# Backward of a transformer block on one Trainium2 core: joined loads, re-timed transposes, another order of the tail

## The chip, the core and the metric

The kernel runs on one core of one Trainium2 chip. The metric is the device time of one execution in microseconds (us). The core has a matrix engine (PE), a vector engine (DVE), an activation engine (ACT), a general engine (POOL) and SP, whose queue issues most of the DMAs here. All five run beside each other and wait for one another by semaphores. Matrix products land in PSUM, which DVE and ACT empty.

## What is computed

The reference is a block y = x + attention(norm(x)) + ffn(norm(x)) and the gradients of all its inputs for a given grad_out. There are 2048 rows of 448 columns, 16 heads of 28 columns, and an FFN of 1792 columns; all is bf16.

```
xn = layernorm(x)
q, k, v = split(xn @ wqkv)
p = softmax(q k^T / sqrt(28));  o = p v
y = x + o @ wo + (silu(xn @ w_gate) * (xn @ w_up)) @ w_down
outputs: y, d/dx, d/dwqkv, d/dwo, d/dw_gate, d/dw_up, d/dw_down
```

Output 1 is the input gradient d/dx, output 2 the gradient of w_qkv.

## The kernel before

A head's 28 columns are padded to 32 (HP), so four heads fill the 128 partitions; such a four is a *group* (G = 4 groups), and half of it, two heads on 64 partitions, is a *pair* (8 pairs). The rows come in 16 tiles of 128 (NT).

**Forward stage** (L255 to L624). Layer norm, then for each group and each block of 512 queries the exponentials of the scores and their product with v; the FFN, its gradients and the next group's projections are queued as filler for PE between the steps, each with a cost, and worked off at an even pace (`fill`, L308). `proj_done` (L198) writes a group's transposed q, k and v to DRAM with three POOL DMAs of 128 partitions. `do` (L496), the tail of a group's block, makes the gradient of the head outputs, divided by the softmax sum, transposes it with a DMA and writes it to DRAM (L524). At the end of the stage `load_pair(0, 1)` and `load_group(0, 1, ...)` bring in what the next stage needs first.

**Backward attention** (L641 to L917) is one loop over 512 *units* and 16 steps more. A unit is one pair, one block of 512 keys (kc) and one tile of 128 queries; eight units are a *window* (UW = 8, window number W, place in it pos). Step k of the loop does, in the order of the code:

- PE: scores of unit k (L851, q's first 64 partitions with k's) and dP of unit k-1 (L862, the last 64 partitions: dO with v). Both go to `sd` tiles, 3 buffers of two PSUM banks.
- ACT: E = exp(scores) (L869). DVE: ds = dP * E (L880), in one of 8 `ds` buffers.
- ds must also be had transposed, as `dsT` of the window. For six of eight units SP issues a DMA transpose (L882). The two units named in TQ (1 and 4) are transposed by PE into the PSUM tile `aux` (`pe_transpose`, L770) and copied out (`tr_out`, L778): unit 1 at pos 6 of its window, with the copy on DVE at once; unit 4 at pos 0 of the next window, with the copy on ACT behind that step's E.
- PE: `acc_mm(k-3)` (L738) adds unit k-3 to the gradients of v and k of the key block; after the last one ACT empties it (L754), SP transposes it (L761), POOL writes it to `dqkv_d` (L763).
- At pos 5, `dq_mm(W-2)` (L784) multiplies the dsT of two windows before with k, into `aux`; at pos 6 DVE adds the result up (`dq_out`, L799). After the fourth key block it is transposed (L817) and written (L820).
- Each window has a *job* for PE, spread over pos 1 to 4 into the single `aux` bank: an output tile of y, a tile of one of the two FFN parts of d/dx (written to pA_d and pB_d), or a part of the w_qkv gradient of a finished group (`dwq_mms`, L669: xn tiles as the stationary operand, the gradients of q, k, v as the moving one, four chunks of 128 columns of d). `job_out` empties it at pos 4. The chunk that a job reads is loaded by SP two windows before, at pos 0 (L660, L666).

Other loads are issued by SP at pos 4 (L840 to L846): from three lists, `pload` (the next pair, eight loads: q, k, dO and v, 64 partitions each, in two halves), `gload` (the next group, six loads) and `wload` (weights), it takes up to 2, 1 and 2 in each window. `load_pair` (L545) fills two tiles of 128 partitions for a pair: q above dO, and k above v.

**Tail** (L898 to L981). The last group's w_qkv gradient is begun at step N + UW + 5 with the key and value products of 12 tiles for four chunks; the rest follows behind the loop, then its q part, each chunk copied out by ACT, packed by POOL and written (L688). Then for each of 16 tiles of d/dx: PE sums pA, pB (L956) and 12 products of the q, k, v gradients with w_qkv (L958); ACT copies it with a row sum (L962), DVE makes the second sum and two scalars bb and cc (L965 to L971), ACT scales it into t1 (L974), DVE adds cc * xn to get t2 (L976), POOL adds grad_out (L979), SP stores it (L980). `load_c` (L929) brings in pA, pB, grad_out and `dqkv_d` by chunks of two or four tiles, first by SP, later by ACT.

Of the kernel before, what the change touches and what calls it, by code (L numbers as in the profile page):

```python
# [17 lines left out]
S = 2048  # L18
# [19 lines left out]
def kernel(  # L38
# [27 lines left out]
    qT_d = dram.tile([G, P, S], BF16, name="qT_d")  # L66
    kT_d = dram.tile([G, P, S], BF16, name="kT_d")
    vT_d = dram.tile([G, P, S], BF16, name="vT_d")
    dOT_d = dram.tile([G, P, S], BF16, name="dOT_d")
# [396 lines left out]
    def o_items(g, qc, o_ps):  # L466
# [29 lines left out]
        def do(i):  # L496
# [27 lines left out]
            pool.dma_start(out=dOT_d[g, :, qc * 512:(qc + 1) * 512], in_=dT[:])  # L524
# [20 lines left out]
    def load_pair(pr, parts):  # L545

        g, r = pr // 2, 64 * (pr % 2)
# [4 lines left out]
        return [lambda i=i, dst=dst, r0=r0, src=src: sp.dma_start(  # L552
                    out=dst[r0:r0 + 64, i:i + n], in_=src[g, r:r + 64, i:i + n])
                for r0, srcs in ((0, (qT_d, kT_d)), (64, (dOT_d, vT_d)))
                for dst, src in zip((q, k), srcs) for i in range(0, S, n)]
# [73 lines left out]
    outp = cst.enter_context(tc.tile_pool(name="outp", bufs=2))  # L629
    ps_sd = cst.enter_context(tc.tile_pool(name="ps_sd", bufs=3, space=PSUM))  # L630
# [137 lines left out]
    TQ = (1, 4)  # L768
# [9 lines left out]
    def tr_out(eng):  # L778

        ps, dst = st["tr"]  # L780
        out, in_ = dst.rearrange("p j c q -> p (j c) q"), ps[:]
        act.copy(out=out, in_=in_) if eng is act else dve.tensor_copy(out=out, in_=in_)  # L782
# [45 lines left out]
    dps = {}  # L828
    fillers, last_dwq = [], []
    for k in range(N + 2 * UW):  # L830
        W, pos = k // UW, k % UW
        if k < N:
            pr, kc, w, qi = units[k]
            if k % 64 == 3 and pr + 1 < NPR:
                pload.extend(load_pair(pr + 1, 2))
            if k % 128 == 3 and pr + 2 < NPR:
                gload.extend(load_group(pr // 2 + 1, 2, vp if pr // 2 % 2 else ksp))
            if pos == 0:
                job_load(W + 2)
            if pos == 4:  # L840
                if W == len(jobs) - 1:
                    wload.extend(load_w("wq", 2))
                for lst, n in ((pload, 2), (gload, 1), (wload, 2)):
                    for f in lst[:n]:
                        f()
                    del lst[:n]  # L846
            q, kv = qd[pr]
            qt = 8 * w + qi
            s_ps = ps_sd.tile([P, 2, 512], FP32, name="sd")
            for j in range(2):  # L850
                pe.matmul(s_ps[:, j, :], lhsT=q[HP * j:HP * j + HP, qt * P:(qt + 1) * P],  # L851
                          rhs=kv[HP * j:HP * j + HP, kc * 512:(kc + 1) * 512],
                          start=True, stop=True, tile_position=(HP * j, 0))
        late_tr = pos == 0 and 1 <= W <= NW
# [15 lines left out]
        if late_tr:  # L870
            tr_out(act)
# [15 lines left out]
        if pos == 1:  # L887
            if 3 <= k < N + 3:
                acc_mm(k - 3)
            if job:  # L890
                st["aux"] = ps_x.tile([P, 512], FP32, name="aux")
                fillers = job_mms(W, st["aux"])
        if 1 <= pos < 5 and job:
            n = -(-len(fillers) // (5 - pos))
            for f in fillers[:n]:
                f()
            fillers = fillers[n:]
        if k == N + UW + 5:  # L898
            for c in range(4):
                if c % 2 == 0:  # L900
                    g_t = ps_sd.tile([P, 2, 512], FP32, name="sd")
                last_dwq.append((g_t[:, c % 2, :], dwq_mms(3, c, g_t[:, c % 2, :])))
            for _, m in last_dwq:
                for f in m[0][:12]:
                    f()
# [3 lines left out]
        if pos != 1 and 3 <= k < N + 3:  # L909
            acc_mm(k - 3)  # L910
        if pos == 4 and job:
            job_out(W, st["aux"])
        if pos == 6 and W < NW:
            pe_transpose(W, TQ[0])
            tr_out(dve)
    while sp_later:
        sp_later.pop(0)()  # L917
    ast.close()


    with ExitStack() as fin:
        ckf = fin.enter_context(tc.tile_pool(name="ckf", bufs=5))
        wk = fin.enter_context(tc.tile_pool(name="wk", bufs=3))
        one = fin.enter_context(tc.tile_pool(name="one", bufs=1))
        dy_t = one.tile([P, NT, D], BF16, name="dy_t")
        pab = [one.tile([P, NT, D], BF16, name=f"pab{i}") for i in range(2)]
        dq_c = {}

        def load_c(ck, q):  # L929

            if ck >= NT // 2:
                return
            if ck % 2 == 0:
                ts = slice(2 * ck, 2 * ck + 4)
                for i, src in enumerate((pA_d, pB_d)):
                    q.dma_start(out=pab[i][:, ts, :], in_=src[:, ts, :])
                act.dma_start(out=dy_t[:, ts, :], in_=dy_d[:, ts, :])
            dq_c[ck] = ckf.tile([P, 3 * G, 2 * P], BF16, name="dq_c")
            q.dma_start(out=dq_c[ck][:], in_=dqkv_d[ck])
        for ck in range(3):  # L940
            load_c(ck, sp)
        for part in range(2):
            for c, (ps, m) in enumerate(last_dwq):
                for f in m[part][12 * (1 - part):]:
                    f()
                if part == 1:
                    dwq_out(3, c, ps)
        wq = wtile["wq"]
        for t in range(NT):
            if t % 2 == 0:  # L950
                load_c(t // 2 + 3, act)
            cks = dq_c[t // 2]
            g_t = ps_sd.tile([P, 2, 512], FP32, name="sd")
            g_ps = g_t[:, 0, :D]
            for i in range(2):
                pe.matmul(g_ps, lhsT=ident_bf[:], rhs=pab[i][:, t, :], start=(i == 0), stop=False)  # L956
            for n in range(3 * G):
                pe.matmul(g_ps, lhsT=cks[:, n, (t % 2) * P:(t % 2 + 1) * P], rhs=wq[:, n, :],  # L958
                          start=False, stop=(n == 3 * G - 1))
# [15 lines left out]
            t2 = wk.tile([P, D], FP32, name="t2")  # L975
            dve.scalar_tensor_tensor(out=t2[:], in0=xn_sp[:, t, :D], scalar=cc[:, 0:1], in1=t1[:],  # L976
                                     op0=ALU.mult, op1=ALU.add)
            dx = wk.tile([P, D], BF16, name="dx")
            pool.tensor_tensor(out=dx[:], in0=t2[:], in1=dy_t[:, t, :], op=ALU.add)  # L979
            sp.dma_start(out=out1_d[:, t, :], in_=dx[:])  # L980
# [31 lines left out]
```

## Time and profile before

| | us |
|---|---|
| three runs | 1529.53, 1534.82, 1534.94; median 1534.82 |
| the profiled execution, its own time | 1534.68 |
| its span (first to last instruction) | 1532.9 |
| forward stage, to about | 645 |
| backward attention, from there to about | 1457 |
| tail, from there to the end | 1532.9 |

| engine | busy us | share of the span |
|---|---|---|
| PE (matrix products) | 1414.2 | 92% |
| ACT | 1187.9 | 77% |
| DVE | 1100.7 | 72% |
| POOL | 395.0 | 26% |

The views read are: sums of busy time over stretches; waits (who waited for whom, in total, number of times, longest); the timeline (start, duration, engine, line, what is written and read, and in brackets the idle time before it and what ended it); and the chain of work that ended last, followed back in time. PE's matmuls are pipelined and their ends modelled, so a PE that is busy 97% may still have waits on the chain. Rows of SP are those of its queue: the time that it takes to issue a DMA, not that of the transfer; how long a transfer took to land is told apart. L numbers are lines of the kernel.

### The profile page before, as it was taken

Reading aid. Unit: us, or ns where it says so; the run is one execution under the profiler, and the core shown is the slowest. Engines: PE = TensorE matmul, PEld = TensorE weight load, DVE = VectorE, ACT = ScalarE, POOL = GpSimd, SP = SyncE. Lnnn points to the kernel's source line nnn. Section 1 sums busy time; section 2 is a strip of 40 time slices with the busy share of each in tenths; the row PEclk is TensorE's granted clock in tenths of the full one; section 3 lists DMA queues with packets and bytes.
Section 4 is the critical chain, followed back from the end, with each engine's and each line's share of the span. In section 5 each row is a group of like instructions: output and inputs, shape, how many; then the busy total and the mean of one; then the engine's idle time right before and its main releaser. Section 6 shows DMA issues by size and latency. Waiting matters only on the chain.

```text
span 1532.9 us, 32019 instructions
## 1 busy us (share of the span) xinstructions
PE 1414.2 (92%) x12176; PEld 600.1 (39%) x12176; DVE 1100.7 (72%) x1421; ACT 1187.9 (77%) x1333; POOL 395.0 (26%) x664
## 2 busy tenths in 40 slices
PE   6899999999999999798989988989899899999987
PEld 3233333333333333333334344334345343544353
DVE  7664555656666667377878878888788788888925
ACT  6898998889888888576767777778778778788823
POOL 4332443344435444400111121101112101111033
PEclk9999999999999999889999999999999999999999
DMA  9976767878877799799999999999999999999984
GB/s 216 190 157 144 156 122 157 171 136 169 173 166 144 159 190 214 178 197 208 218 206 207 185 194 209 197 204 206 208 195 197 198 205 183 180 190 211 186 272 140
DMA packets 682106, 285.12 MB, mean 186 GB/s; under 512 B 637136, under 2 KB 650464, under 8 KB 681952
## 3 DMA queue, kind: packets, MB, share of 16 engines
q1 hardware_dynamic: 652016, 210.03, 75.5%
q0 software_dynamic: 25968, 64.53, 17.2%
q10 hardware_dynamic: 3968, 8.52, 1.7%
q8 instruction: 95, 1.56, 0.4%
q14 instruction: 59, 0.48, 0.1%
HBM read 67.34 MB, written 63.44 MB: 85 GB/s over the span
## 4 chain that ended last, share of the span: by engine, by line
PE 59%; ACT 13%; DMA 12%; DVE 8%; issue 6%; POOL 1%; SPq 0%; DVEq 0%; ACTq 0%; POOLq 0%
DMA dsT<-ds 9%; PE f_ps L356 8%; PE s_ps L599 7%; PE f_ps L382 7%; PE sd L851 6%; ACT E L869 5%; PE aux L718 5%; PE acc L748 4%; PE o_ps L581 4%; ACT eT L604 4%; PE aux L775 4%; DVE ds L880 4%; PE aux L795 3%; ACT dsT L782 3%; PE f_ps L180 3%
## 5 line engine op out<-in xcount | busy, mean ns | idle before, releaser
L880 DVE TENSOR_TENSOR ds<-sd,E 128x1024 bf16<-128x1024 f32 x512 | 611.5, 1219 | 134.0 <-PE sd L862 49.8
L869 ACT ACTIVATE E<-sd 128x1024 bf16<-128x1024 f32 x512 | 516.7, 1023 | 175.6 <-PE sd L862 136.5
L604 ACT ACTIVATE eT<-s_ps 128x1024 bf16<-128x1024 f32 x512 | 497.2, 1025 | 79.5 <-PE s_ps L599 76.1
L862 PE MATMUL sd<-kT,qT 32*128 32x512 bf16 x1024 | 203.4, 390 | 22.2 <-ACT E L869 21.3
L851 PE MATMUL sd<-kT,qT 32*128 32x512 bf16 x1024 | 202.7, 392 | 20.6 <-DVE ds L880 18.0
L748 PE MATMUL acc<-ds,v_sp 128*32 128x512 bf16 x1024 | 205.3, 396 | 0.7 <-DVE ds L880 0.7
L748 PE MATMUL acc<-E,O_sp 128*32 128x512 bf16 x1024 | 205.1, 396 | 0.2 <-ACT dkv_o L754 0.2
L599 PE MATMUL s_ps<-qT,kT 32*128 32x512 bf16 x1024 | 152.8, 383 | 10.1 <-ACT eT L604 7.9
L421 POOL DMA_DIRECT2D hd_d<-fT x168 | 126.9, 773 | 18.5 <-DVE fT L416 5.3
L382 PE MATMUL f_ps<-xnT,wgu 128*128 128x512 bf16 x448 | 117.6, 381 | 1.7 <-DVE w_sb L408 1.5
L763 POOL DMA_DIRECT2D dqkv_d<-dkv_o x64 | 39.2, 616 | 293.3 <-ACT dkv_o L754 291.4
L718 PE MATMUL aux<-W,ck 128*128 128x448 bf16 x448 | 107.5, 357 | 3.3
L851 PEld LDWEIGHTS <-qT 32*128 32x128 bf16 x1024 | 51.2, 91 | 150.0 <-issue 141.2
L581 PE MATMUL o_ps<-eT,v_sp 128*32 128x512 bf16 x1024 | 102.8, 391 | 0.0
L356 PE MATMUL f_ps<-xn_sp,f_sp 128*128 128x448 bf16 x448 | 99.7, 356 | 0.0
L599 PEld LDWEIGHTS <-kT 32*128 32x128 bf16 x1024 | 42.4, 90 | 143.5 <-issue 136.8
L748 PEld LDWEIGHTS <-O_sp 128*32 128x32 bf16 x1024 | 50.3, 93 | 113.5 <-issue 104.0
L775 PE MATMUL aux<-ident_bf,ds 128*128 128x128 bf16 x1024 | 81.3, 224 | 13.5 <-DVE dq_acc L807 6.5
L356 PEld LDWEIGHTS <-f_sp 128*128 128x128 bf16 x672 | 58.3, 98 | 78.6 <-issue 23.5
L862 PEld LDWEIGHTS <-qT 32*128 32x128 bf16 x1024 | 65.2, 91 | 60.5 <-issue 56.5
L775 PEld LDWEIGHTS <-ds 128*128 128x128 bf16 x1024 | 63.5, 99 | 42.4 <-issue 41.7
L394 DVE SCALAR_TENSOR_TENSOR g<-t_sb,f_ps 128x512 f32<-128x512 f32 x56 | 38.4, 686 | 54.0 <-ACT t_sb L392 53.9
(133 smaller groups left out, 1763.1 us busy)
## 6 DMA issues: line engine op xcount, KB each, us to landing
hd_d<-fT POOLq DMA_DIRECT2D x168, 128.0 KB, 4.6
ck<-hd_d SPq DMA_DIRECT2D x32, 448.0 KB, 4.3
ck<-hd_d SPq DMA_DIRECT2D x16, 576.0 KB, 4.9
dsT<-ds SPq DMA_TRANSPOSE x384, 4.2
dqkv_d<-dkv_o POOLq DMA_DIRECT2D x64, 64.0 KB, 3.8
dq_c<-dqkv_d ACTq DMA_DIRECT2D x5, 768.0 KB, 6.1
W<-wT_d SPq DMA_DIRECT2D x14, 224.0 KB, 3.6
out_dram<-dw_o POOLq DMA_DIRECT2D x28, 96.0 KB, 3.7
```

Source lines behind the costliest of these rows:

```text
L356: pe.matmul(acc[:, :D], lhsT=src[:, 12 * (t // 4) + 4 * wi + t % 4, :], rhs=rhs[:, t, :D], start=(t == 0), stop=(t == NT - 1))
L382: pe.matmul(st[name][:], lhsT=w(c), rhs=src[:, tsl, c, :], start=(c == 0), stop=(c == 3))
L581: pe.matmul(o_ps[HP * hh:HP * (hh + 1), :], lhsT=v[:, kt, HP * hh:HP * (hh + 1)], rhs=e[hh // 2][:, hh % 2, :], start=(kt == 0), stop=(kt ...
L599: pe.matmul(s_ps[:, j, :], lhsT=kT[r:r + HP, kt * P:(kt + 1) * P], rhs=qT[r:r + HP, qc * 512:(qc + 1) * 512], start=True, stop=True, tile_ ...
L604: act.activation(out=e[:], in_=s_ps[:], func=ACT.Exp, scale=SCALE)
L718: return [lambda n=n: pe.matmul(ps[:, :D], lhsT=t[:, n, :], rhs=w[:, n, :], start=(n == 0), stop=(n == NFC - 1)) for n in range(NFC)]
L748: pe.matmul(acc[r:r + HP, :], lhsT=src[:, qt, 64 * hp + HP * j:64 * hp + HP * j + HP], rhs=m[:, j, :], start=(qt == 0), stop=(qt == NT - 1 ...
L775: pe.transpose(ps[:, i, :], ds[:, i // 4, (i % 4) * P:(i % 4 + 1) * P], ident_bf[:])
L851: pe.matmul(s_ps[:, j, :], lhsT=q[HP * j:HP * j + HP, qt * P:(qt + 1) * P], rhs=kv[HP * j:HP * j + HP, kc * 512:(kc + 1) * 512], start=Tru ...
L862: pe.matmul(d_ps[:, j, :], lhsT=q[r:r + HP, qt * P:(qt + 1) * P], rhs=kv[r:r + HP, kc * 512:(kc + 1) * 512], start=True, stop=True, tile_p ...
L869: act.activation(out=E[k][:], in_=s_ps[:], func=ACT.Exp, scale=SCALE)
L880: dve.tensor_tensor(out=DS[k - 1][:], in0=d_ps[:], in1=E[k - 1][:], op=ALU.mult)
```

## The change

Four places, beside each other in one diff:

1. **Copies and loads of pairs.** The DRAM tensors qT_d, dOT_d, kT_d and vT_d become two, laid out by pair as the loads want them: qdo_d (q above dO) and kv_d (k above v). `proj_done` writes them with six DMAs of 64 partitions for three of 128, `do` with two for one. `load_pair` takes four loads of 128 partitions instead of eight of 64. At pos 4 the loop takes one pair load in even windows and one group load in odd ones.
2. **Transposes by PE.** TQ becomes (2, 6). Unit 2 is still transposed at pos 6, its copy comes a step later, at pos 7 behind ds; unit 6 is transposed at pos 1 of the next window, and DVE copies it ahead of ds. ACT copies no dsT any more.
3. **The job** begins at pos 2 and is spread over three positions instead of four.
4. **The tail.** The last w_qkv gradient is made with the operands exchanged: the gradients of q, k, v are the stationary operand, xn (448 columns) the moving one, so that three PSUM tiles hold it transposed; three DMA transposes turn it back, POOL packs it with five copies, four DMAs write it. Its Q part (64 products of 32 columns in four strips) comes behind the first two tiles of d/dx. pA and pB of the first four tiles are loaded in the last window, chunk 0 of dqkv_d right behind the loop. In the loop over tiles, t2, the addition of grad_out and the store of a tile come one tile later (`finish`), and the last three additions run on DVE.

The diff, cut to its core:

```diff
-    qT_d = dram.tile([G, P, S], BF16, name="qT_d")
...
+    qdo_d = dram.tile([2 * G, P, S], BF16, name="qdo_d")
+    kv_d = dram.tile([2 * G, P, S], BF16, name="kv_d")
...
-        pool.dma_start(out=vT_d[g], in_=vT[:])
-        pool.dma_start(out=qT_d[g], in_=qT[:])
-        pool.dma_start(out=kT_d[g], in_=kT[:])
+        for hp in range(2):
+            rows = slice(64 * hp, 64 * hp + 64)
+            for dst, src in ((kv_d[2 * g + hp, 64:], vT), (qdo_d[2 * g + hp, :64], qT), (kv_d[2 * g + hp, :64], kT)):
+                pool.dma_start(out=dst, in_=src[rows, :])
...
-        return [lambda i=i, dst=dst, r0=r0, src=src: sp.dma_start(
-                    out=dst[r0:r0 + 64, i:i + n], in_=src[g, r:r + 64, i:i + n])
-                for r0, srcs in ((0, (qT_d, kT_d)), (64, (dOT_d, vT_d)))
-                for dst, src in zip((q, k), srcs) for i in range(0, S, n)]
+        return [lambda i=i, dst=dst, src=src: sp.dma_start(out=dst[:, i:i + n], in_=src[pr, :, i:i + n])
+                for i in range(0, S, n) for dst, src in ((q, qdo_d), (k, kv_d))]
...
-    TQ = (1, 4)
+    TQ = (2, 6)
...
+                if W == NW - 1:
+                    load_sums(0, sp, prep)
...
-                for lst, n in ((pload, 2), (gload, 1), (wload, 2)):
+                for lst, n in ((pload, 1 - W % 2), (gload, W % 2), (wload, 2)):
...
-        late_tr = pos == 0 and 1 <= W <= NW
+        late_tr = pos == 1 and 1 <= W <= NW
...
-            tr_out(act)
+            tr_out()
...
+        if pos == 7 and W < NW:
+            tr_out()
+        acc = 3 <= k < N + 3
+        if pos == 2 and job:
+            st["aux"] = ps_x.tile([P, 512], FP32, name="aux")
+            fillers = job_mms(W, st["aux"])
+        lump = []
+        if 2 <= pos < 5 and job:
             n = -(-len(fillers) // (5 - pos))
+            lump, fillers = fillers[:n], fillers[n:]
...
+        def kv(t):
+            pe.matmul(ps, lhsT=dsp[2 * G - 2 + c][0][:, t, :], rhs=xn_sp[:, t, :D],
+                      start=(t == 0), stop=(t == NT - 1))
+
+        def q(t):
+            for h in range(4):
+                pe.matmul(ps[HP * h:HP * (h + 1)],
+                          lhsT=dsp[2 * G - 2 + h // 2][1][:, t // 8, t % 4, t % 8 // 4,
+                                                          HP * (h % 2):HP * (h % 2 + 1)],
+                          rhs=xn_sp[:, t, :D], start=(t == 0), stop=(t == NT - 1),
+                          tile_position=(0, HP * h), skip_group_check=True)
...
+        for t in range(2):
+            dx_mms(t, first[t])
+        q_t = ps_sd.tile([P, 2, 512], FP32, name="sd")
+        for f in last_dwq(2, q_t[:, 0, :D]):
+            f()
...
+            add = pool if t < NT - 3 else dve
+            add.tensor_tensor(out=dx[:], in0=t2[:], in1=dy_t[:, t, :], op=ALU.add)
+            sp.dma_start(out=out1_d[:, t, :], in_=dx[:])
...
+            if t > 0:
+                finish(t - 1, *held)
+            held = (t1, cc)
+        finish(NT - 1, *held)
```

More of the change, by code (lines that the diff above doesn't have):

```diff
@@ L523, in do @@
                                    in_=dOl[:].rearrange("p t c -> p (t c)"))
-            pool.dma_start(out=dOT_d[g, :, qc * 512:(qc + 1) * 512], in_=dT[:])
+            for hp in range(2):
+                pool.dma_start(out=qdo_d[2 * g + hp, 64:, qc * 512:(qc + 1) * 512],
+                               in_=dT[64 * hp:64 * hp + 64, :])
         push([[(0.2, lambda i=i: tr(i)) for i in range(4)], [(0.26, lambda i=i: do(i)) for i in range(4)]]
@@ L924 @@
         one = fin.enter_context(tc.tile_pool(name="one", bufs=1))
+        one3 = fin.enter_context(tc.tile_pool(name="one3", bufs=3))
         dy_t = one.tile([P, NT, D], BF16, name="dy_t")
[L926 to L931, printed above, removed]
-                return
[L933 to L948, printed above, removed]
-        for t in range(NT):
[L950 to L959, printed above, removed]
+        z = one.tile([P, 4, 3, 4, DH], BF16, name="dwq_z3")
@@ new lines, in dx_mms @@
+        def dx_mms(t, g_ps):
+            for i in range(2):
+                pe.matmul(g_ps, lhsT=ident_bf[:], rhs=pab[t // 4, i][:, t % 4, :], start=(i == 0), stop=False)
+            for n in range(3 * G):
+                pe.matmul(g_ps, lhsT=dq_c[t // 2][:, n, (t % 2) * P:(t % 2 + 1) * P], rhs=wq[:, n, :],
+                          start=False, stop=(n == 3 * G - 1))
+        load_dy(0)
+        for ck in range(1, 4):
+            load_dq(ck, sp, ckf)
+        load_sums(1, sp, one3)
+        for c, (ps, m) in enumerate(last):
+            for f in m[12:]:
+                f()
+            last_out(c, ps)
```

98 lines of the change are left out of this document (64 added, 34 removed).

## The prediction

> **What bounds the kernel now.** I read the stage sums first, then the waits of the backward stage, one disturbed and one quiet window in the timeline, the chain through a quiet window, and the tail. The backward stage has 64 windows of 8 units; a window's length is the distance between every eighth L880 row. It has three parts:
>
> ```profile
> 657.20:870.80 213.60, 196.25 (x1828) 82.24 (x1824) 168.83 (x160) 155.31 (x168) 22.49 (x38) 0.98 1.10 207
> 870.80:1290.30 419.50, 381.52 (x4020) 172.90 (x4016) 349.96 (x331) 320.92 (x346) 58.06 (x130) 0.98 1.08 200
> 1290.30:1445.70 155.40, 149.02 (x1620) 68.89 (x1616) 138.25 (x132) 126.14 (x137) 22.50 (x54) 0.99 1.09 190
> ```
>
> The columns are stretch, length, then busy PE, PEld, DVE, ACT and POOL. The third part (13 windows) runs at 11.95 us a window with PE busy 96%; quiet windows of the first part, whose PE job is longer, take 12.51. At those paces the first part (16 windows) would take 200.2 and the second (33) 394.4; they take 13.4 and 25.1 more. So 38.5 us are lost in windows that have something the others lack: loads of the next pair and group. The waits of that stage say who is late:
>
> ```profile
> DVE ds L880 <- DMA dsT<-ds: 46.6, 33, 3.6
> ```
>
> VectorE waits 46.6 us for transposes of old ds tiles (there are 8 buffers). One such place:
>
> ```profile
> 978.90 1.26 SPq L882 DMA_TRANSPOSE dsT<-ds  x1
> ...
> 980.25 0.53 SPq L666 DMA_DIRECT2D ck<-hd_d  x1
> ...
> 980.88 5.90 SPq L882 DMA_TRANSPOSE dsT<-ds  x3
> ...
> 986.75 1.23 DVE L880 TENSOR_TENSOR ds<-sd,E 128x1024 bf16<-128x1024 f32 x1 [1.42 <-DMA dsT<-ds]
> 986.83 1.66 SPq L552 DMA_DIRECT2D kT<-kT_d  x2
> 988.02 0.39 PE L851 MATMUL sd<-kT,qT 32*128 32x512 bf16 x2 [0.50 <-DVE ds L880]
> ```
>
> The SP queue has no gap: it is the queue that is behind. Comparing each L882 row's start with the end of the L880 row that it serves, SP lags 1 to 4 us in quiet windows, climbs to 8 in windows with pair loads, stalls VectorE there, and then works off about 1 us a window. Its work in a window at 1.36 us a transpose (start to start): 6 transposes 8.2, the transposes of dkv_o and dq_o 1.0 on average, the chunk load 0.6, held up in a row some 1 to 2: about 11.0 of 11.95. Each half-partition pair load adds 0.62, two in each of four windows; a group load adds 0.62 in six. That is more than the 0.9 left.
>
> In a quiet window the chain goes through PE and two ACT waits:
>
> ```profile
> 1373.37 1.02 ACT dsT L782
> 1374.38 0.04 issue
> 1374.43 0.92 PE aux L718 x4
> ...
> 1383.09 1.03 ACT E L869
> ...
> 1384.55 0.57 PE aux L775 x8
> 1385.12 0.02 issue
> 1385.14 1.02 ACT dsT L782
> ```
>
> The PE job of each window waits for ACT's copy of transposed ds.
>
> **The loads.** Before: 8 pair loads in the first four windows of a pair, two each, and 6 group loads, one a window. After: 4 pair loads, one in every even window, and 6 group loads in the odd ones. A load of 128 partitions by 2 KB is not in L552, but the group loads move 256 KB in one row: 0.58 us of SP, landing in 3.6. So SP's extra work falls from at most 1.9 us a window to at most 0.62, and SP gets 11.6 to do in 11.95 (12.1 with the x_c load, in 12.5). Bounds for the 38.5: all stays (if bytes, not rows, are the limit: they are the same) or all goes. I take three quarters, **-29**: the lag already falls by 1 us in a window that has 0.9 to spare. The last pair load is issued two windows before its use, with 3.6 us to land. In the forward stage POOL gets 12 + 16 more DMA rows of 0.53 to 0.62 us, 16 us in 640, where it is busy 270; PE (97%) covers it, nobody reads these tensors for 100 us. Uncovered it would cost the 16; I take 0.
>
> The Trainium skill, "DMA: Bandwidth & Descriptors", section "Rules for kernel authors", also says that two transfers to disjoint partition halves serialize and that one of 128 partitions should be used. Its section "Issuing engines are not separate DMA queues" speaks against a large gain: issue time on a sequencer is usually small relative to the DMA itself. By that the -29 would be near 0 and the time about 1522 (rival 2). The gapless SP row is against it here.
>
> **The transposes in PE.** The second one moves to position 1 of the next window, both are copied by DVE: 62 copies of 1.01 us leave ACT, 62 of 0.68 join DVE. In the row of three ds, 3.47 us, DVE takes one each 1.125 us and a copy 0.60 (1383.11 to 1383.71). DVE's own work rises from 8 x 1.125 + 0.6 + 0.6 = 10.2 to 10.8 of 11.95. PE's stays: positions without a job 0.66 (two pairs of score products 0.33, four accumulations 0.33), transposes 0.57, dQ products 1.15, the job 14 x 0.187 plus 0.12 a lump. I laid these out by hand, with PE allowed ahead until the three sd slots stop it: the order before gives 11.46, the new one 11.25 (E to product waits remain; the job waits for a copy that DVE has finished half a us before). PE's job in three lumps instead of four leaves DVE more bunched: positions 6, 7, 0, 1 hold 6.3 us of DVE work against 3.8 of PE. So a window is 6.76 (positions 2 to 5) + 6.3 - B, where B is how far DVE may lag behind PE; my layout has B near 1.8. Bounds for 62 windows: +37 (each 0.60 uncovered) to -50 (a copy wait of 0.8 gone each). By the layout -13; since SP's 11.0 to 11.6 is then close behind, I take half, **-6**. Other PE-transposed units (2, 6 for 1, 4) leave six DMA transposes in a window, as before.
>
> **The tail.** The chain before:
>
> ```profile
> 1458.92 4.89 DMA dsT<-ds
> 1463.86 1.05 PE aux L795 x14
> 1464.93 0.70 DVE dq_o L813
> 1465.65 6.62 DMA dq_sp<-dq_o
> 1472.32 0.97 PE sd L681 x15
> ```
>
> PE is idle 4.8 us for dq_sp, then works off 128 products with copies between them, and begins the input gradient at 1479.4. New: two sums (896 KB) are loaded in window 63, in front of the last transposes; at the 256 GB/s of this stretch up to 3.5 us, I take 2.5, so the last dQ products end at 1467.4 for 1464.9. Then 8 kv products (448 wide, 0.19): 1468.9. The first tile needs dq_c of chunk 0: its last write lands at 1463.6, its load takes 4.5 to 8.1 us (rows of dq_c), so 1470.5. Two tiles at 2.65: 1475.8; dq_sp has landed by then (3.5 to 6.6 us after 1468.1). The Q part, 64 products in four column strips: between 3.0 (four at once, 16 x 0.19) and 12.2 (one by one); the row L795, 16 in 1.15 us at 512 wide, gives 4.0: 1479.8. Then 14 tiles.
>
> ```profile
> 1483.46 0.15 DVE L969 SCALAR_TENSOR_TENSOR bb<-s,rstd 128x1 f32<-128x1 f32 x1
> ...
> 1518.33 1.03 POOL L979 TENSOR_TENSOR dx<-t,dy_t 128x448 bf16<-128x448 f32 x1 [1.70 <-DVE t L976]
> ...
> 1518.71 0.67 DVE L969 SCALAR_TENSOR_TENSOR bb<-s,rstd 128x1 f32<-128x1 f32 x1
> 1519.30 0.15 DVE L971 SCALAR_TENSOR_TENSOR cc<-s,rstd 128x1 f32<-128x1 f32 x1
> 1519.47 0.72 ACT L974 ACTIVATE t<-sd,bb,rstd 128x448 f32<-128x448 f32 x1 [1.48 <-DVE cc L971]
> ```
>
> While POOL adds, the tiny bb takes 0.67 instead of 0.15 and ends with it: add, bb, t1, t2, add is a ring of 2.73 us, longer than PE's 2.65, and it throttles PE by its sd slots. With t2 and the add held back a tile, POOL's add lies beside ACT's t1, the ring is about 2.4, PE sets 2.65: 14 x 2.65 = 37.1, PE ends at 1516.9 (before: 1523.05). Behind it 1.7 (g_sb, junk, bb, cc), 1.3 (t2 and add of tile 14), 1.3 (the last, add on DVE; bounds 0.6 and 1.03 by t2 and POOL's add), 2.5 for the store as now: 1523.7, against 1532.9. That is -9; POOL's new copies (between 0.18, the row of 56 elements, and 1.03 each, five of them) and four stores wait for the transposed Q part and hold tiles 1 to 3 back, I take **-7**; bounds -10 and +2 (Q part uncovered, loads late).
>
> **Sum**: profiled execution 1534.7 (span 1532.9 and 1.8 around it; the median shown is 1534.8): -29 - 6 - 7 = **1493**. Own range 1478 to 1510.
>
> **Rivals.** 1. *VectorE becomes the bound (slower).* If B is under 0.3, because every ds waits for its own product, a window is about 12.9 instead of 12.57 (788.5 us over 62 windows, less what the longer jobs add). With B = 0.1: 62 x (12.96 - 12.57) = +24, no stalls left to save, tail -7: 1552. The point is B = 0.4: below it the windows cost more than the tail gives. For it: DVE's busy share of 89%; against it: ds rows back to back with PE ahead by a unit. Chance 0.08.
> 2. *Bytes, not rows, hold SP.* The same bytes bring the same stalls: 1534.7 - 6 - 7 = 1522. For it: DMA share over 1 everywhere and an L882 row of 3.2 us with its ds ready; against it: windows with one extra load at the end of the stage run at 11.95. Chance 0.13.
> 3. *Gains and DVE cancel.* B near 0.5: windows as long as now on the mean, tail -7: 1528. Chance 0.10.
> 4. *More*: the layout's -13 and all 38.5 come through with the tail's -9: 1474 or less. Chance 0.05. That loads are not joined at all is not one: the new slice spans all partitions.
> Forecast 0.64.
>
> **Numbers.** A measurement of this kernel tells about 0.5% from no change: under 1527 is faster. Forecast, 2 and 4: 0.82. Case 3: 0.10. Case 1: 0.08. The range 1474 to 1528 leaves out rival 1 and most of rival 4.
>
> **What would show it.** Loads: the wait of ds for dsT falls from 46.6 to under 15, SP's lag stays under 6, windows of the second part near 11.9. Transposes: no dsT copy on ACT, quiet windows 11.6 to 11.9; if they are over 12.2, DVE is the bound. Tail: first dx product near 1470 in old time, bb at 0.15, tiles each 2.65. I am wrong if ds still waits for dsT, or if PE waits for ds in quiet windows.

## The result and the profile after

| | before | after |
|---|---|---|
| median of the runs | 1533.2 us | 1513.6 us (1511.0, 1511.1, 1516.2, 1516.7) |
| ratio, 95% interval | | 0.9876 [0.9844, 0.9908] |
| profiled execution, span | 1534.7, 1532.9 us | 1511.0, 1509.2 us |
| last copy of the forward stage, to the first ds | 2.2 us | 10.7 us |
| the same copy, to SP's first dsT transpose | 10.4 us | 12.0 us |
| windows 1 to 62 | 788.5 us | 760.2 us |
| tail, from the start of window 63 | 87.2 us | 84.7 us |

The change brings 19.6 us (23.7 in the profiled executions) where 42 were forecast. The same three parts of the backward stage as before (windows 1 to 16, 17 to 49, 50 to 62), same columns, kernel after:

```profile
664.30:868.20 203.90, 193.15 (x1832) 79.17 (x1828) 178.03 (x177) 142.26 (x152) 22.55 (x38) 0.99 1.10 210
868.20:1273.70 405.50, 369.07 (x4020) 161.13 (x4020) 367.57 (x364) 288.87 (x312) 58.20 (x130) 0.99 1.10 207
1273.70:1424.50 150.80, 141.75 (x1624) 64.41 (x1620) 144.79 (x144) 113.52 (x123) 22.55 (x54) 1.00 1.10 198
```

Lengths of 213.6, 419.5 and 155.4 us became 203.9, 405.5 and 150.8. ACT lost the copies, DVE gained them, and DVE is now busy 144.8 of 150.8 us in the last, quiet part. Quiet windows with a dx job take 11.55 us (before: 11.95), those with a dwq job 11.75, with a y job 12.49. At those paces, and with windows 17 and 50 at their measured lengths, the 62 windows would take 733 (16 x 12.49, 12 x 11.75, 32 x 11.55 and 2 x 11.11), so 27 us are still lost in disturbed ones (before: 38.5). Not all of that is the loads': without any loads 9 us are lost too (742.0 us, below). The wait that names them, from the waits of the same stage:

```profile
DVE ds L903 <- DMA dsT<-ds: 21.5, 22, 3.1
```

It was 46.6 us. The chain through a quiet window of the kernel after, around the late PE transposes:

```profile
1362.22 0.61 PE aux L774 x8
1362.83 0.32 PE sd L874 x2
1363.15 0.06 PE sd L885 x2
1363.21 1.01 ACT E L892
1364.27 0.39 PE sd L885 x2
```

No dsT copy on ACT is left in it; the PE transposes (L774) lead straight into score products (L874), and one ACT E remains where there were an E and a copy. The start of the stage, on DVE and on SP:

```profile
651.94 5.75 DVE L903 TENSOR_TENSOR ds<-sd,E 128x1024 bf16<-128x1024 f32 x5 [10.07 <-DMA out_dram<-dwd_sb]
...
653.20 2.62 SPq L905 DMA_TRANSPOSE dsT<-ds  x2
```

This is new: the first ds waits 10.07 us for the store of a forward tile, and then five come back to back. And the tail, on ACT, POOL and PE:

```profile
1460.48 0.33 ACTq L835 DMA_DIRECT2D dq_c<-dqkv_d  x1
1460.86 0.54 ACT L1025 ACTIVATE g_sb<-sd 128x448 bf16<-128x448 f32 x1 [13.02 <-DMA pab<-pA_d]
...
1464.15 1.71 POOL L966 COPY dwq_z<-dwq_o 128x224 bf16<-128x224 bf16 x4 [16.74 <-DMA dwq_o<-dwq_t]
...
1465.06 0.90 PE L977 MATMUL sd<-pab,ident_bf 128*128 128x448 bf16 x2 [6.60 <-ACT t L1037]
```

PE had the first two tiles and the Q part done at 1455.6, but the first g_sb, which empties tile 0, stands in ACT's queue behind a load (the row of 1460.48, issued 9.6 us after the load ahead of it), and POOL's additions stand behind a copy that waits for a transpose; so PE waits 6.60 us for a slot. The wait costs more than its length. Behind it the profile's granted clock is 0.50 for 5.1 us (1.00 before and after), and the products of that tile take twice the time of the next tile's (the first row against the second):

```profile
1465.76 4.68 PE L979 MATMUL sd<-W,dq_c 128*128 128x448 bf16 x12
...
1470.75 2.43 PE L979 MATMUL sd<-W,dq_c 128*128 128x448 bf16 x12
```

That is another 2.7 us, 9.3 with the wait.

### The profile page after: what moved, and what is told of

The parts are those of the page before. It is cut to its first block, busy times and chain, and to the rows that moved or that the text cites. A ratio compares the mean times of both kernels' runs of the same rounds, so it can differ in the third digit from the quotient of the medians.

```text
span 1509.2 us, 31495 instructions
## 1 busy us (share of the span) xinstructions
PE 1389.1 (92%) x12016; PEld 573.1 (38%) x12016; DVE 1132.2 (75%) x1488; ACT 1128.2 (75%) x1268; POOL 406.7 (27%) x673
## 4 chain that ended last, share of the span: by engine, by line
PE 68%; DVE 10%; ACT 9%; DMA 8%; issue 4%; SPq 1%; DVEq 0%; POOL 0%; ACTq 0%; POOLq 0%
PE sd L874 8%; PE f_ps L355 8%; PE s_ps L597 7%; PE acc L747 7%; PE f_ps L381 6%; PE aux L717 5%; ACT E L892 4%; PE aux L774 4%; DMA dsT<-ds 4%; PE o_ps L579 4%; PE aux L711 4%; DVE ds L903 4%; ACT eT L602 4%; PE sd L885 3%; PE aux L792 3%
## 5 line engine op out<-in xcount | busy, mean ns | idle before, releaser
L874 PE MATMUL sd<-kT,qT 32*128 32x512 bf16 x1024 | 201.0, 388 | 14.9 <-DVE ds L903 8.2
L874 PEld LDWEIGHTS <-qT 32*128 32x128 bf16 x1024 | 52.4, 91 | 143.3 <-issue 135.4
L717 PE MATMUL aux<-W,ck 128*128 128x448 bf16 x448 | 101.4, 355 | 0.0
L774 PE MATMUL aux<-ident_bf,ds 128*128 128x128 bf16 x1024 | 79.4, 221 | 14.8 <-DVE dq_acc L807 5.2
L779 DVE COPY dsT<-aux 128x1024 bf16<-128x1024 bf16 x128 | 87.2, 681 | 0.7 <-PE aux L774 0.7
## 6 DMA issues: line engine op xcount, KB each, us to landing
dq_c<-dqkv_d ACTq DMA_DIRECT2D x5, 768.0 KB, 6.1
```

The lines of the kernel that those rows point to most:

```text
L717: return [lambda n=n: pe.matmul(ps[:, :D], lhsT=t[:, n, :], rhs=w[:, n, :], start=(n == 0), stop=(n == NFC - 1)) for n in range(NFC)]
L774: pe.transpose(ps[:, i, :], ds[:, i // 4, (i % 4) * P:(i % 4 + 1) * P], ident_bf[:])
```

## The experiments

Each row is from the kernel's own profile in us, but for the time: median, and the ratio to runs of the kernel before on the same chip. "ds" and "transpose" are the start of the first one behind the start of the forward stage's last copy (dwd_sb). The forward stage itself ended between 638.1 and 648.2 in executions with nearly the same forward code, so stages tell more than spans.

| kernel | median | ratio [95%] | ds | transpose | windows 1-62 | tail |
|---|---|---|---|---|---|---|
| before | | 1 | 2.2 | 10.4 | 788.5 | 87.2 |
| after | 1513.6 | 0.9876 [0.9844, 0.9908] | 10.7 | 12.0 | 760.2 | 84.7 |
| after_again | 1514.6 | 0.9842 [0.9796, 0.9888] | 10.3 | 11.6 | 766.3 | 84.8 |
| before_joined | 1525.5 | 0.9943 [0.992, 0.9965] | 2.2 | 10.5 | 773.1 | 85.3 |
| before_tq | 1531.4 | 0.9982 [0.996, 1.0004] | 2.2 | 10.9 | 783.6 | 89.2 |
| after_noloads | 1495.4 | 0.9743 [0.9716, 0.977] | 9.9 | 11.2 | 742.0 | 85.2 |
| after_tiny | 1508.5 | 0.9829 [0.9799, 0.9859] | 9.7 | 11.0 | 756.6 | 84.7 |
| after_poolq | 1519.8 | 0.992 [0.9895, 0.9945] | 9.8 | 11.1 | 768.0 | 84.6 |
| after_actq | 1512.9 | 0.9876 [0.9824, 0.9927] | 10.5 | 11.8 | 756.6 | 85.8 |
| after_actck | 1555.9 | 1.0151 [1.0105, 1.0197] | 11.1 | 12.3 | 802.7 | 87.4 |
| after_pools | 1518.7 | 0.9915 [0.9883, 0.9947] | 2.2 | 11.0 | 775.4 | 87.6 |
| after_pools2 | 1512.7 | 0.9859 [0.9832, 0.9887] | 2.2 | 11.8 | 771.6 | 87.6 |
| after_pools3 | 1518.6 | 0.991 [0.988, 0.994] | 2.2 | 10.6 | 769.0 | 97.0 |
| after_pools4 | 1519.2 | 0.989 [0.9855, 0.9926] | 2.2 | 3.8 | 759.1 | 97.6 |
| after_tail | 1513.7 | 0.9866 [0.9834, 0.9897] | 10.5 | 11.7 | 762.7 | 83.0 |
| after_tail2 | 1507.1 | 0.9848 [0.9787, 0.991] | 10.8 | 12.0 | 760.8 | 76.1 |
| after_best | 1512.1 | 0.9828 [0.9785, 0.987] | 10.8 | 12.0 | 762.8 | 81.4 |
| after_best4 | 1498.0 | 0.9754 [0.9715, 0.9793] | 2.2 | 3.8 | 757.0 | 79.7 |

### The scatter: the changed kernel again

> The changed kernel itself, for the scatter on one chip: windows 1 to 62 within 3 us of 760.3 and tail within 2 us of 84.7, if the differences told between the kernels are to mean anything; time 1511 to 1517.

The windows are 6.1 us longer than in the first profile and the tail equal: windows scatter by twice what was expected. Differences of under 6 us in windows of one profile are taken for nothing below.

### The parts alone

before_joined is the kernel before with part 1:

```diff
-                for lst, n in ((pload, 2), (gload, 1), (wload, 2)):
+                for lst, n in ((pload, 1 - W % 2), (gload, W % 2), (wload, 2)):
```

> The kernel before with part 1 alone (joined copies and loads, one pair load in even windows, one group load in odd ones). Theory R (the SP queue's rows are what the disturbed windows wait for): with the old window of 11.95 us and SP's work of 11.0 to 11.6 the 38.5 us of disturbed windows shrink to under 10, the wait of ds for dsT from 46.6 to under 10, time near 1534 - 30 = 1504. Theory B (bytes): the bytes are the same, the wait stays near 46 us, time 1534. Theory N (the two gains do not add: each alone would bring more than its share of the joint change, because a shorter window leaves SP no slack again): as R here, 1504.

before_tq is the kernel before with parts 2 and 3 (`TQ = (2, 6)`, both copies on DVE, the job in three positions), the tail and the loads as before:

```diff
-    TQ = (1, 4)
+    TQ = (2, 6)
...
-            tr_out(act)
+            tr_out()
```

> The kernel before with parts 2 and 3 alone (which units PE transposes, both copies on DVE, the job in three positions). Quiet windows 11.55 us for 11.95, as in the changed kernel. Theory N: loads still go in two halves, SP has 11.0 to 12.9 us of work in a window of 11.55, so the disturbed windows lose more than before (over 50 us) and the time is 1534 - 17 + 15 = 1532. Theory B, or if the two gains add: disturbed windows lose the same 38.5, time 1534 - 17 = 1517.

Joined loads alone: 0.9943 of the time before, -8.7 us by the ratio, interval -12.3 to -5.4 (-15.4 in the windows of its profile), not -30. The wait of ds for dsT is hardly shorter than the 46.6 us before:

```profile
DVE ds L878 <- DMA dsT<-ds: 44.1, 35, 3.2
```

Theories R and N had the gain too large, B too small. Quiet windows of this kernel still last as long as before, so by the forecast's reckoning SP had 11.6 us to do in 11.95 and the stalls should have gone; they did not. What fell is the row time itself: in windows 1 to 62 SP has 45 rows of loads for 71, which take 29.6 us for 49.3, and the windows are 15.4 us shorter. SP's rows still fill 93% of them, as before. The transposes alone: quiet windows of 11.54 us, as forecast for the changed kernel, but 1 to 62 only 4.9 us shorter: of 17 us that the quiet pace gives (750 to 733), 12 go into longer stalls (the wait of ds for dsT is 50.2 us). That is what theory N said of this part: SP, which has no gap, takes back what a shorter window gives. That the two parts do not add is not shown: -15.4 - 4.9 is about what the whole change brings in windows less its start (below).

### Rows or bytes

after_noloads:

```diff
-                pload.extend(load_pair(pr + 1, 2))
+                qd[pr + 1] = qd[0]
...
-                gload.extend(load_group(pr // 2 + 1, 2, vp if pr // 2 % 2 else ksp))
+                spt[pr // 2 + 1] = spt[0]
```

> The changed kernel without the pair and group loads of the backward stage: all pairs work on the first pair's q, k, dO, v, so that the gradients of the other pairs are not computed; neither the rows nor the bytes of 52 loads (13 MB) are left. Both theories: with nothing that only the disturbed windows have, the windows with a dx job run at 11.55 us, those with a y job at 12.49, and the 27 us that are still lost go: 1513.6 - 24 = 1490. If windows are still disturbed, the loads are not the cause, but the DMA transposes and the chunk loads themselves (theory D: the 16 DMA engines are full with what every window has): then 1505 or more.

after_tiny issues the same loads into tiles that are not read, with `dst[:, i:i + m]`, m = n // 16, and one tile of a group load's eight (an eighth of its bytes, not a sixteenth). The loads of the stage are 46 (7 pairs by 4, 3 groups by 6; 11.8 MB), not the 52 of the expectations:

> As the kernel without loads, but each of the 52 loads is still issued with a sixteenth of its bytes, into tiles that nobody reads (the gradients of all pairs but the first are not computed). Theory R (SP's rows): as many rows as in the changed kernel, so the disturbed windows stay, 1513. Theory B (bytes on the DMA engines hold SP in its rows): a sixteenth of the bytes is almost nothing, as without loads, 1490.

The waits of the stage, first without loads, then with a sixteenth to an eighth of their bytes:

```profile
DVE ds L903 <- DMA dsT<-ds: 5.1, 6, 1.5
```

```profile
DVE ds L910 <- DMA dsT<-ds: 24.4, 30, 2.0
```

Without loads 5.1 us are left of 21.5; with their rows and almost no bytes the wait is as long as with all (24.4). In windows: 742.0 without loads, 756.6 with rows and few bytes, 760.2 and 766.3 with all. So of 18 to 24 us that the loads still cost, 14.6 come with 46 loads that move almost nothing, and 4 to 10, hardly more than the scatter, with the bytes. Against theory B, most of the cost is not bytes. That it is the time of SP's rows, as theory R says, is not shown by this: the small loads are still transfers that the DMA engines carry out, as many as before. The next section takes the rows off SP.

One figure speaks against a reason that the prediction gave for rival 2 (bytes hold SP in its rows): I summed what each dsT transpose's SP row takes beyond 1.23 us once its ds is ready. It is 113.7 us over the stage before, 117.1 after, 111.7 without loads. Rows are held up, but not by these loads as long as SP issues them.

### Another queue for the loads

after_poolq, and with `act` for `pool` after_actq:

```diff
-                pload.extend(load_pair(pr + 1, 2))
+                pload.extend(load_pair(pr + 1, 2, pool))
...
-        return [lambda i=i, dst=dst, src=src: sp.dma_start(out=dst[:, i:i + n], in_=src[pr, :, i:i + n])
+        return [lambda i=i, dst=dst, src=src: lq.dma_start(out=dst[:, i:i + n], in_=src[pr, :, i:i + n])
```

> The changed kernel with the pair and group loads of the backward stage issued from POOL's queue instead of SP's; the same bytes in the same windows. Theory R or N: SP has 10.5 us of work a window, the 27 us that the disturbed windows still lose fall below 10, the wait of ds for dsT from 21.5 to under 8, time 1513.6 - 18 = 1495. Theory B: bytes and their order are the same, the wait stays at 21 us, time 1513.

> The changed kernel with the pair and group loads of the attention stage issued from ACT's queue. From POOL's queue they brought no gain (windows 1 to 62 768.0 us for 760.3), though SP had fewer rows. Theory R (SP's rows hold the disturbed windows; POOL's queue is another kind of queue that is slow by itself): stalls shrink to those of the kernel without loads plus the bytes, windows 1 to 62 near 750, time 1513.6 - 10 = 1504, less what 0.6 us on ACT cost where ACT is late. Theory B (rows grow by the bytes in flight, whoever issues them): windows near 760 or more, 1513 to 1520.

after_actck:

```diff
-            sp.dma_start(out=t[:], in_=hd_d[j[1], :, :G + NFC, :])
+            act.dma_start(out=t[:], in_=hd_d[j[1], :, :G + NFC, :])
...
-            sp.dma_start(out=x[:], in_=x_d[:, j[1], :])
+            act.dma_start(out=x[:], in_=x_d[:, j[1], :])
```

> The changed kernel with the chunk loads (ck, x_c: a row of 0.57, in the first part another of 0.43 us, in nearly every window) issued from ACT's queue instead of SP's. Theory R: SP has 0.6 to 1.0 us less to do in each window, more than the loads of pairs on the mean, stalls fall from 27 to under 12, time 1513.6 - 13 = 1500, less ACT's own rows where ACT is late (at most 56 x 0.6 = 34). Theory B: no change in the stalls, 1513 or more.

POOL's queue: 768.0, no gain; windows 2 to 12 then all take 12.4 to 12.5 us, but windows 40 to 43 lose 15 us. The same loads land later from there (the DMA issues of windows 17 to 49: O_sp 7.3 us in the median for 3.4, qT 5.3 for 3.5). ACT's queue: 14.4 us are lost in windows 17 to 49 for 22.5 and 25.5, but 7.1 for 4.0 and 4.8 in windows 1 to 16; together within the scatter, and the time is that of the changed kernel.

So theory R fails in this form: 30 us of load rows leave SP's queue, and no time clear of the scatter comes back. SP's rows in windows 1 to 62 still add up to 715.0 us (loads on POOL) and 703.9 (on ACT), for 707.2 and 708.6 in the two profiles of the changed kernel, because the transposes' rows are longer: by the sum above they take 152 and 144 us beyond 1.23 each, for 117. A transpose's row is thus no fixed cost: beside loads from another queue the transposes' rows grow by about what the load rows had taken. Neither theory fits all runs, R not these two and B not after_tiny. What holds the rows stays open.

Chunk loads on ACT: 42 us slower. Undisturbed y windows in which ACT issues two such loads (rows of 0.33 and about 0.46 us) last 13.6 us for 12.49; the y windows 14 to 16, without a load, last 12.49, and dx windows with one row 11.55 to 11.6, as without. So one row on ACT was hidden, and two were paid with more than their length. Theory R's 1500 left that out.

### The start of the stage

Four orders of the SBUF pools; nothing else changes but the chunk 0 load of the tail, which from the second on goes to the pool ckf behind the loop. after_pools and after_pools2:

```diff
+    dsw = ast.enter_context(tc.tile_pool(name="dsw", bufs=8))
+    ework = ast.enter_context(tc.tile_pool(name="ework", bufs=5))
     ckp = ast.enter_context(tc.tile_pool(name="ckp", bufs=3))
     ksp = ast.enter_context(tc.tile_pool(name="ksp", bufs=1))
-    ework = ast.enter_context(tc.tile_pool(name="ework", bufs=5))
-    dsw = ast.enter_context(tc.tile_pool(name="dsw", bufs=8))
```

after_pools3:

```diff
+    dsw = ast.enter_context(tc.tile_pool(name="dsw", bufs=8))
+    twin = ast.enter_context(tc.tile_pool(name="twin", bufs=3))
+    ework = ast.enter_context(tc.tile_pool(name="ework", bufs=5))
     ckp = ast.enter_context(tc.tile_pool(name="ckp", bufs=3))
     ksp = ast.enter_context(tc.tile_pool(name="ksp", bufs=1))
-    ework = ast.enter_context(tc.tile_pool(name="ework", bufs=5))
-    dsw = ast.enter_context(tc.tile_pool(name="dsw", bufs=8))
-    twin = ast.enter_context(tc.tile_pool(name="twin", bufs=3))
```

> The changed kernel with the SBUF pools of the attention stage opened in another order (dsw, ework, ckp, ksp, twin, dqa), so that the ds buffers no longer lie over the forward stage's temporary tiles. Theory A (the 10.07 us wait of the first ds for the store of dwd_sb comes from the address: the new pool of 13.3 KB pushed ds upwards over that buffer): the first ds comes at about 645 instead of 652, time 1513.6 - 7 = 1506.5. Theory F (the forward stage ends later, by its additional copies): the first ds stays near 652, time 1513.6.

> The changed kernel with the pools in the order dsw, ework, ckp, ksp, twin, dqa and chunk 0 of the last stage outside the pool prep, so that now neither the ds buffers nor the chunk buffers lie over the forward stage's temporary tiles (in the first try SP was held by the chunk load instead, until 655, and windows 1 and 2 took 5.7 us more). First ds about 1.6 us behind the forward's last copy as in the kernel before, first chunk load at once, windows 1 and 2 near 12.5: 1513.6 - 7 = 1506.

> The changed kernel with the pools in the order dsw, twin, ework, ckp, ksp, dqa (chunk 0 of the last stage outside prep), so that neither ds nor the first two dsT lie over the forward stage's dwd_sb. Theory A (the start of the attention stage waits for that store by address, first at ds, and with ds moved at SP's first transpose, at 649.85, whose lag of 8 us then cost 11 us in the windows): first transpose about 2 us behind the first ds, lag of window 0 under 2, start of windows 7 us earlier with windows as in the changed kernel: 1513.6 - 8 = 1506. Theory D (what is won at the start is lost in the windows anyway, because the DMA engines have a fixed sum of work): 1513.

after_pools4, in addition:

```diff
     op_ = fst.enter_context(tc.tile_pool(name="op_", bufs=1))
+    fout = fst.enter_context(tc.tile_pool(name="fout", bufs=2))
...
-                o = ftmp.tile([P, D], BF16, name="dwd_sb")
+                o = fout.tile([P, D], BF16, name="dwd_sb")
...
-                    o = ftmp.tile([P, 4, P], BF16, name="dw_o")
+                    o = fout.tile([P, 4, P], BF16, name="dw_o")
```

> As after_pools3, and dwd_sb and dw_o, whose stores land last in the forward stage, in a pool of their own at the top, so that no pool with a late store lies under ds and dsT. Theory P (the wait is for the pool that lay there, not for the one tile): first transpose 2 us behind the first ds, lag of window 0 under 2, and the 7 us stay: 1513.6 - 8 = 1506. Theory D (a fixed sum of DMA work takes them back): windows 1 to 62 near 768 and 1513.

Kernel after_pools2, DVE and SP:

```profile
640.31 1.22 DVE L903 TENSOR_TENSOR ds<-sd,E 128x1024 bf16<-128x1024 f32 x1 [1.59 <-ACT E L892]
...
649.85 2.61 SPq L905 DMA_TRANSPOSE dsT<-ds  x2
```

Kernel after_pools4, the same two:

```profile
648.13 1.22 DVE L904 TENSOR_TENSOR ds<-sd,E 128x1024 bf16<-128x1024 f32 x1 [1.59 <-ACT E L893]
...
649.69 5.11 SPq L906 DMA_TRANSPOSE dsT<-ds  x2
```

In after_pools2 ds comes at once but its first transpose 9.5 us later; in after_pools4 the transpose follows in 1.6. So theory A was right that the wait comes from what lies below, and wrong about what: in after_pools3 neither ds nor the first dsT lie over dwd_sb (worked out from the pools' order and sizes), and still the transposes waited; only when the late tiles left the pool ftmp did they start (theory P). The new pool prep (13.3 KB) had pushed dsw up over ftmp; before, only twin lay over it. That explains why the wait is old: before, SP began 8.2 us behind ds and worked that off in the first windows (windows 1, 3, 4 and 5 together are 7.4 us over the quiet pace, with loads in them too); after, DVE waits and SP starts in step. First ds plus windows 1 to 62 is 790.7 before, and 770.9 and 776.6 after, 773.8 and 771.2 in after_pools2 and 3: the order of the pools moves the wait and keeps the sum. In after_pools4 it is 761.3, so the 10 to 15 us were to be had, against theory D. Its time is not shorter, since its tail took 97.6: three PE waits of 13.8 us together for ACT's t, behind POOL, as in the next section, and 4.8 us more in slow products behind two of them.

### The tail

after_tail moves ACT's loads behind the tile's two ACT instructions, a tile later:

```diff
-            if t % 4 == 0 and t // 4 + 1 < 4:
...
             held = (t1, cc)
+            if t % 4 == 1 and t // 4 + 1 < 4:
```

> The changed kernel with ACT's loads of the last stage (grad_out, pA, pB, chunks of dqkv) issued one tile later and behind that tile's two ACT instructions instead of ahead of them. Theory Q (ACT's queue stands behind a load that waits, so the first tile's g_sb comes 13 us late and holds PE by its slots): g_sb of tile 0 comes at once, PE goes on after the Q part at 2.65 us a tile, the tail is 5 to 9 us shorter: 1513.6 - 7 = 1506. Theory L (PE's own loads are late because the transfers of 5 MB take until 1464): no change.

after_tail2 in addition packs the Q part later and stores it from SP:

```diff
-                last_out(2, q_t[:, 0, :D])
+                q_o = last_out(2, q_t[:, 0, :D])
...
+            if t == 7:
+                last_pack(2, q_o)
```

> As after_tail (ACT's loads a tile later, behind its two instructions), and the last pack of the w_qkv gradient (one POOL copy, four stores) not at tile 2 but behind tile 7, its stores from SP's queue instead of POOL's. Theory Q2 (in after_tail PE ran at 2.65 us a tile until tile 7 and then stood 5.35 us, because POOL waited 5.87 us for the transposed Q part and then 4 us in its four stores, with the additions of tiles 1 to 5 queued behind them): no wait of PE over 1 us in the loop, end of PE 36 us after the Q part, tail 5 to 7 us shorter than the changed kernel's 84.7: 1513.6 - 6 = 1507. Rival (another queue takes POOL's place, SP's stores for instance): 1513.

after_tail gained 1.7 us, not 7: g_sb came on time, PE ran at 2.65 us a tile to tile 8 (counted from 0), and then waited all the same. POOL and PE of after_tail:

```profile
1473.13 0.56 POOL L966 COPY dwq_z<-dwq_o 128x448 bf16<-128x448 bf16 x1 [5.87 <-DMA dwq_o<-dwq_t]
1473.98 1.49 POOL L971 DMA_DIRECT2D out_dram<-dwq_z  x2 [0.29 <-POOL dwq_z L966]
1477.07 1.34 POOL L971 DMA_DIRECT2D out_dram<-dwq_z  x2 [1.60 <-issue]
...
1483.41 0.91 PE L977 MATMUL sd<-pab,ident_bf 128*128 128x448 bf16 x2 [5.35 <-ACT t L1031]
```

From the end of one addition to the next POOL spends 11 us: 5.87 of waiting for the transposed Q part, then one copy and four stores. The additions behind them hold DVE's t2 buffers, these ACT's t, that PE's slots. With the pack behind tile 7, PE of after_tail2:

```profile
1456.60 3.21 PE L845 MATMUL sd<-xn_sp,dq_sp 128*32 128x448 bf16 x64
...
1494.56 2.43 PE L983 MATMUL sd<-W,dq_c 128*128 128x448 bf16 x12
```

14 tiles in 37.2 us from the end of the Q part with no wait, and a tail of 76.1 (-8.6). The 6.9 us to after_tail's tail are its wait of 5.35 and 1.7 in the slow products behind it. Theory Q2 holds in this profile, and ACT's queue was only the first of two. The median alone would not show it: the ratio 0.9848 [0.9787, 0.991] is no different from that of the changed kernel.

### Together

after_best is after_tail2 with the edit of after_actq, after_best4 the same with that of after_pools4.

> after_tail2 and after_actq in one: if the two gains add (8.7 us in the tail, 3.7 in the windows), the time is 1513.6 - 12 = 1501; if ACT's loads only helped by chance of one profile, as after_tail2, 1506.

> after_best with the pools of after_pools4: under theory P another 7 us less, 1494; under D as after_best, 1501.

after_best did not add up: 1512.1, its tail 81.4. The loads on ACT brought nothing again. Of the 5.3 us by which its tail is longer than after_tail2's, 4.1 are one PE wait of 2.58 us and 1.5 in slow products behind it: ACT stood 5.79 us for its load of grad_out, with g_sb behind it. So ACT's queue can still hold the loop, and the -8.6 of after_tail2 is one profile's; the same tail gained 3.4 here and 5.1 in after_best4 (there PE waits 1.73 us for dq_c, and slow products take 1.4). after_best4 is the fastest kernel: 1498.0 us against 1514.6 of the changed kernel on the same chip, by start (-8.1), windows (-9.3) and tail (-5.1), less a forward stage that ended 2.6 us later in this execution.

## Why the prediction was right about the sign and wrong about the size

- **The loads, forecast -29: the step that failed.** "I take three quarters" of 38.5, because SP's work, 11.6 us at most, would fit into a window of 11.95. Part 1 alone, in windows of that length, measured -8.7, with the wait of ds for dsT still at 44.1 us. The step assumed a threshold, below which SP comes free and the stalls go; part 1 met it on paper and they stayed. What the runs showed in its place is a gain no larger than the row time that went away (19.7 us of rows, windows 15.4 shorter). With the second step the windows shrank to 11.55, and the 46 joined loads still cost 18 to 24 us, 14.6 of them with almost no bytes; without any loads 9 us stay lost. The reckoning also took a transpose's row as a fixed cost, and these rows grew by some 30 us in sum when the loads came from another queue. What holds them stays open, and with it how a load comes to stall a window.
- Some of the 38.5 us (up to 7.4, in the first windows) went with SP's late start and not with the loads alone: after_pools4, where SP starts in step, is 5.0 us shorter in windows 1 to 16 than after_pools3.
- By the prediction's own signs it was wrong: ds still waits for dsT, 21.5 us and not under 15; SP's lag, forecast under 6 us, still climbs to 9; the middle windows take 12.3 on the mean and not 11.9. The time lies between the forecast and rival 2 (1522), which had all stalls stay.
- **The Trainium skill**, "DMA: Bandwidth & Descriptors", section "Issuing engines are not separate DMA queues", says that issue time is usually small relative to the DMA. Here an L905 row takes 1.23 us, where the transpose lands in 4.3 (median), and six of them fill 64% of a window: not small. But the gain near 0 that followed from this sentence came closer to the -8.7 than the -29 did.
- **The transposes, forecast -6.** The quiet window fell to 11.55, by 0.40: -17 over the 62 windows, somewhat more than the hand layout's -13, and neither ds wait nor copy is on the chain shown. The halving for SP was right in kind: alone, this part measured -2.8 [-6.1, +0.6], which is not clear of nothing. VectorE did not become the bound (rival 1), though it is busy 96% of the last part.
- Together, start and windows were forecast at -35 and measured -14 to -20 (790.7 to 770.9 and 776.6). That windows 1 to 62 alone fell by 28.3 us in the first profile is no confirmation: 8.5 of it moved to the start, and up to 6 may be scatter.
- **The start, forecast nothing.** The prediction did not look at what lies under the new pool's address; +8.5 at the first ds, mostly given back because SP then starts in step.
- **The forward stage, forecast 0.** Right as far as can be seen: the last copy came at 642.28 in before_joined and 642.59 before, but the scatter of 10 us hides anything small.
- **The tail, forecast -7, measured -2.5.** Behind the start of window 63 the first dx product came after 22.6 us (1447.1 - 1424.5; forecast 1470.5 - 1445.7 = 24.8), and the Q part took 3.21 us (forecast 4.0): right, also the end 6.8 us behind PE (1502.41, where the last g_sb starts, to 1509.2). Wrong was "hold tiles 1 to 3 back" as a small term: ACT's loads and the POOL queue made PE wait 6.60 us, and the slow products behind the wait took 2.7 more; without both, after_tail2's tail is 8.6 us shorter. bb is 0.15 to 0.16 in most tiles, but 0.33 to 2.10 in four, beside additions on POOL.

## What to carry to other kernels

A saving on a full queue was worth no more here than the row time that it removed: do not expect the stalls to vanish because the sum of rows now fits, and cost the rows against the new, shorter window. Test whether a row is the queue's own work before moving it to another queue; here what left one row came back in others. Before an allocation is added ahead of others, look which earlier pool now lies under each tile of the next stage: here, as far as one pair of kernels shows, the first writer waited for the last reader of that whole pool. And on an engine that issues DMAs in order with its work, place what must wait (stores, loads into buffers in use, packs behind a transpose) behind what others wait for. And count a wait of PE as more than its length (9.3 us for 6.60 here).

## What the runs showed of the hardware

- The 64 products of 32 columns in four column strips take 3.21 us, about 16 x 0.19: four strips ran at once.
- PE waits of 1.73 to 8.14 us in the tail's loop (16 of them, over all profiles with the changed tail but after_tail2's) were each followed by dx products 0.37 us apart instead of 0.19, 7 to 16 times, at a granted clock of 0.50; that cost 1.2 to 2.9 us more. After the ten waits of 0.34 to 1.24 us the clock was 1.00 and the products came 0.19 apart.
- The same 256 KB loads land in 4.4 to 7.3 us from POOL's queue and in 3.2 to 4.0 from SP's (medians in windows 17 to 49).
- SP's transposes are held in their rows by 112 to 134 us in a stage of 780 by the sum above, whether the loads are there or not, and by 143 to 155 where ACT or POOL issues loads beside them; by what, the runs do not tell.
